# Seven block products instead of eight in both products of an MLP, with partial sums read out of PSUM between them

## The chip, the cores and the metric

One NeuronCore of a Trainium2 chip. The metric is the device time of one execution in microseconds. The kernel before takes 619.16 us (median of three runs, 618.53 to 621.18). Engines are called as the profile calls them: PE (TensorE), PEld (its weight loads), DVE (VectorE), ACT (ScalarE), POOL (GpSimd), SP (the queue that issues most transfers).

## The reference

An attention-like recurrence with a state of 48 x 48 for each head, followed by an MLP with a hardswish gate:

```python
# r, k, v, w: (4, 8, 768, 48) float32;  u: (8, 48)
for t in range(S):
    cur = einsum('bhd,bhe->bhde', u[None] * kt, vt)
    y[:, :, t] = einsum('bhd,bhde->bhe', rt, state + cur)
    state = wt[:, :, :, None] * state + einsum('bhd,bhe->bhde', kt, vt)

x = y.transpose(0, 2, 1, 3).reshape(3072, 384)
h = x @ w_in                                # (384, 2048)
g = h * clip(h + 3.0, 0.0, 6.0) / 6.0
out = g @ w_out                             # (2048, 384)
```

The MLP weights arrive as 64-bit floats and are converted to 32-bit floats on the chip. All products run in fp32.

## The kernel before

**Attention.** The 3072 tokens are 24 chunks of L = 128. For each chunk DVE runs two scans over the decays (`back_scan` L329, `fore_scan` L338); K and R are multiplied in by DVE for the first three chunks and by POOL afterwards (L349, L353). PE forms the scores (`score`, L384) into a PSUM tile of two banks, DVE copies the part above the diagonal into A (`above`, L390), PE reads state and values into another tile of the same kind (`read`, L435 and L452) and forms the state's update (L445). ACT takes the result out of PSUM (`leave`, L505 and L506) into xT, the transposed input of the MLP: three slices of 128 rows by the block's tokens. The fourth pair of heads goes through x3 and six small transfers (`last_pair`); in block 0 it goes through a product with a selection matrix instead (`read_last`, `read_rest`, L482).

**MLP.** BC = 3 chunks make a block (384 tokens, 8 blocks). `up` (L520) multiplies one of 16 slices of w_in (128 of the 2048 columns, three slices of depth) with the block's tokens: three products of 384 columns into one of three "mm" banks. ACT forms relu(h/6 + 1/2) from PSUM (`ramp`, L527), DVE takes min(r, 1) * h (`gate`, L534) into g. `down` (L542) multiplies, for each chunk, 16 slices of g with w_out: 16 products of 384 columns into an mm bank. ACT copies it out (`drain`, L548), SP stores it. Block 0 runs its up products in two parts, first for two chunks (256 columns) and then for one (128). Every fp32 product is two PE instructions in the profile, each with its own weight load.

**Start.** Weights come in 16 fetches of 768 KB (8 pairs of slices of w_in, then 8 of w_out). ACT does two and DVE three conversion steps for each (L298, L302, L307, L312, L317). Until the first up product PE is fed with products of the identity that nobody reads (`spin`, L743).

**Order.** The schedule is written by the program itself. `Plan.add` takes a step's name, engine, assumed duration, the steps that it comes after, a due time (key) and the ring buffers that it holds with the steps that free them. `Plan.order` walks through time: at each turn the engine that can start earliest takes, of its steps that are ready then, the one with the smallest key. The instructions are emitted in that order, and on the chip each engine works through its own list in it; waits follow from the data. A flag marks steps that use the SBUF port shared by DVE and POOL; the plan puts these one after the other. `START`, `CONV`, `UP`, `LAG` and `BEHIND` are the due times of the first chunks, of the conversion, of block 0's up products, the lead of a chunk before its block, and the fetches that the first chunks' loads stand behind. Later steps re-read inputs and check their ranges on DVE (`vet`); a second, general path runs only if such a check fails.

Of the kernel before, what the change touches and what calls it, by code (L numbers as in the profile page):

```python
# [30 lines left out]
UP = (-38.7, 1.8, -33.2, 2.0)  # L31
# [148 lines left out]
def fast_path(tc, feat, tok, wflat, ub, moe_w_in, moe_w_out, out, flag, n_chunks):  # L180
# [13 lines left out]
    MB = BC * L  # L194
    NB = NT // BC
# [3 lines left out]
    with ExitStack() as ctx:  # L199
# [12 lines left out]
        half = const.tile([128, 1], F32, name="half")  # L212
        ones = const.tile([128, 1], F32, name="ones")
        mask_f = const.tile([128, L], F32, name="mask_f")
# [5 lines left out]
        sel = const.tile([PR, NCC, 128], F32, name="sel")  # L220
        x3_0 = const.tile([PR, MB], F32, name="x3_0")
# [3 lines left out]
        def constants():  # L225
# [5 lines left out]
            nc.vector.memset(half, 0.5)  # L231
            nc.vector.memset(ones, 1.0)
            make_identity(nc, ident)

            nc.gpsimd.memset(mask_f, 1.0)
# [3 lines left out]

            nc.gpsimd.memset(x3_0, 0.0)  # L240
# [8 lines left out]
        plan.ring("tok", 4)  # L249
# [12 lines left out]
        def load_tok(i):  # L262
            b = io.tile([L, 3, HD], F32, name="tok_in", bufs=4)
            nc.sync.dma_start(out=b.rearrange("s c e -> s (c e)"), in_=tok[i].rearrange("s c e -> s (c e)"))
            st[i].update(rt=b[:, 0], kt=b[:, 1], v=b[:, 2].rearrange("s (h d) -> s h d", d=D))
# [55 lines left out]
        for r, k in (("E", 3), ("W", 3), ("rk", 2), ("dg", 2), ("A", 2), ("kn", 2), ("S", 2), ("x", 2), ("two", 2),  # L321
                     ("ps", 1), ("mm", 3), ("r6", 3), ("g", NFC + 3), ("o", 2)):
            plan.ring(r, k)
        w_min = const.tile([PR, NT, P], F32, name="w_min")

        def back_scan(i):
            d = st[i]
            E_ = wk.tile([PR, P * (L + 1)], F32, name="E", bufs=3)
# [6 lines left out]
        def fore_scan(i):  # L335
            d = st[i]
            W_ = wk.tile([PR, P * (L + 1)], F32, name="W", bufs=3)
# [20 lines left out]
        def own(i):  # L358
            d = st[i]
            d["rk"] = wk.tile([L, HD], F32, name="rk")  # L360
# [17 lines left out]
        def score(i):  # L378
            d = st[i]
            d["a_ps"] = pp.tile([128, 2, P, L], F32, name="two", bufs=2)  # L380
            for p in range(P):
                for g in range(2):
                    rows = slice(g * GP, g * GP + D)
                    nc.tensor.matmul(d["a_ps"][:, g, p, :], lhsT=d["K"][rows, p, :], rhs=d["R"][rows, p, :],  # L384
                                     start=True, stop=True)

        def above(i):

            d = st[i]
            nc.vector.copy_predicated(  # L390
                out=d["A"].rearrange("s (p g) t -> s g p t", g=2),
                mask=mask.rearrange("s (o x t) -> s o x t", o=1, x=1).to_broadcast([L, 2, P, L]),
                data=d["a_ps"])
# [61 lines left out]
        def new_y(i):  # L455
            st[i].update(started=set(), y_ps=pp.tile([128, 2, P, L], F32, name="two", bufs=2))
# [13 lines left out]
        def leave_last(i):  # L470
            if i == 0:
                blocks[0]["xT"] = wk.tile([128, NCC, MB], F32, name="xT")
            for g in range(2):
                rows = slice(g * GP, g * GP + D)
                nc.scalar.copy(out=x3_0[rows, i * L:(i + 1) * L], in_=st[i]["y_ps"][rows, 1, 0, :])

        def read_rest(i):
            d = st[i]
            begun = set()
            for j in range(NCC):  # L480
                bank, at = PLACES[j]
                nc.tensor.matmul(d["y_ps"][:, bank, at, :], lhsT=sel[:, j, :], rhs=x3_0[:, i * L:(i + 1) * L],  # L482
# [11 lines left out]
        def leave(i):  # L494
            bk, c = divmod(i, BC)
            b = blocks[bk]
            if c == 0:
                b["xT"] = wk.tile([128, NCC, MB], F32, name="xT")
                b["x3"] = wk.tile([PR, MB], F32, name="x3")
# [15 lines left out]
        def up(bk, f, c0, c1):  # L515
            b = blocks[bk]
            cols, m = slice(c0 * L, c1 * L), (c1 - c0) * L
            h_ps = b["h", f, c0] = pp.tile([128, MB], F32, name="mm", bufs=3)
            for j in range(NCC):
                nc.tensor.matmul(h_ps[:, :m], lhsT=w_in[:, f // 2, j, f % 2, :], rhs=b["xT"][:, j, cols],  # L520
                                 start=(j == 0), stop=(j == NCC - 1))

        def ramp(bk, f, c0, c1):
            b = blocks[bk]
            m = (c1 - c0) * L
            r6 = b["r", f, c0] = wk.tile([128, MB], F32, name="r6", bufs=3)
            nc.scalar.activation(out=r6[:, :m], in_=b["h", f, c0][:, :m], func=ACT.Relu, bias=half, scale=1.0 / 6.0)  # L527

        def gate(bk, f, c0, c1):
            b = blocks[bk]  # L530
            cols, m = slice(c0 * L, c1 * L), (c1 - c0) * L
            if c0 == 0:
                b["g", f] = wk.tile([128, MB], F32, name="g", bufs=NFC + 3)
            nc.vector.scalar_tensor_tensor(out=b["g", f][:, cols], in0=b["r", f, c0][:, :m], scalar=1.0,  # L534
                                           in1=b["h", f, c0][:, :m], op0=ALU.min, op1=ALU.mult)

        def down(bk, c, f0, f1):
            b = blocks[bk]
            if f0 == 0:
                b["o", c] = pp.tile([L, DM], F32, name="mm", bufs=3)  # L540
            for f in range(f0, f1):
                nc.tensor.matmul(b["o", c], lhsT=b["g", f][:, c * L:(c + 1) * L], rhs=w_out[:, f, :],  # L542
                                 start=(f == 0), stop=(f == NFC - 1))

        def drain(bk, c):
            b = blocks[bk]
            b["y", c] = wk.tile([L, DM], F32, name="o", bufs=2)
            nc.scalar.copy(out=b["y", c], in_=b["o", c])  # L548

        def store(bk, c):  # L550
            t0 = bk * MB + c * L
            nc.sync.dma_start(out=out[t0:t0 + L, :], in_=blocks[bk]["y", c])
# [13 lines left out]
        def refetch(which, j):  # L566
            if which == "w":
                t = io.tile([128, VN], F32, name="bits", bufs=3)
                nc.sync.dma_start(out=t, in_=wflat[:, j * VN:(j + 1) * VN])
            else:  # L570
                m = VN // 2
                t = io.tile([128, m], I64, name="bits", bufs=3)
# [42 lines left out]

        PB = NFC + BC * 4
        SUBS = ("", ".", "..")[:len(SPLIT) + 1], ("",)

        def when(i):

            bk, c = divmod(i, BC)
            return PB * bk - LAG - PB / BC * (BC - 1 - c)

        for i in range(NT):
            t = when(i)
            k = START[i] if i < len(START) else t - 14
# [8 lines left out]
            plan.add(f"back{i}", "DVE", 1.4, do(back_scan, i), [f"feat{i}"] + [f"fore{i - 2}"] * (i > 1), k,  # L635
# [12 lines left out]
            plan.add(f"diag0{i}", "ACT", 1.22, do(diagonal, i, 0), [f"sum{i}"], k + 0.6, [("A", [f"read{i}"])])  # L648
            plan.add(f"diag1{i}", "ACT", 1.22, do(diagonal, i, 1), [f"sum{i}", f"diag0{i}"], k + 0.6)

            due = k + 0.7 if i <= len(START) else when(i - 1) + 0.02
            t = k + 1 if i < len(START) else t
            plan.add(f"score{i}", "PE", 1.05, do(score, i), [f"K{i}", f"R{i}"], due, [("two", [f"above{i}"])])
            plan.add(f"above{i}", "DVE", 1.3, do(above, i), [f"score{i}", f"diag1{i}"], due + 0.5)
# [12 lines left out]
            space = [("x", [f"up{bk}.{f}{x}" for f in range(NFC) for x in SUBS[bk > 0]])] if c == 0 else []  # L667
            if bk == 0:
                plan.add(f"first{i}", "PE", 0.35 + 0.3 * (not first), do(read_last, i), [f"above{i}"] + reads[2:], t + 0.01,
                         [("two", [f"leave{i}"])])  # L670
                plan.add(f"third{i}", "ACT", 0.55, do(leave_last, i), [f"first{i}"], t + 0.01, space)
# [3 lines left out]
            else:  # L675
                plan.add(f"read{i}", "PE", 1.0 + 0.45 * turn + 0.5 * (not first), do(read, i), reads
                         + [f"up{j}.{NFC - 1}{SUBS[j > 0][-1]}" for j in (bk - 2,) if j >= 0],
                         t + 0.01, [("two", [f"leave{i}"])] + [("ps", [f"state{i}"])] * turn)
                plan.add(f"leave{i}", "ACT", 1.46, do(leave, i), [f"read{i}"], t + 0.5, space)
                if c == BC - 1:  # L680
                    for g in range(2):
                        plan.add(f"move{bk}.{g}", "SP", 1.8, do(last_pair, bk, 0, BC, g, nc.sync),
# [399 lines left out]
```

## Time and profile before

| | |
|---|---|
| median of three runs | 619.16 us |
| the profiled execution | 618.55 us, its span 616.7 us |
| PE busy | 602.4 us, 98% of the span |
| PE busy in L520 and L542 (up, down) | 254.7 and 251.6 us |
| DVE, ACT, POOL busy | 270.7, 215.6, 126.5 us |
| mean granted clock of PE | 0.997 |

How to read it: the page gives busy time by engine, forty slices of the span with the busy share in tenths, and the chain of work that ended last. A row of a group has the line, the engine, the operation, the tiles, the shape, the count, then the busy time and the mean of one instruction, then the idle time of the engine just before it and what ended that. PE's records overlap, since a product's record is longer than the distance to the next one: a price for PE is read from a run of products without a gap, not from the mean of a record.

### The profile page before, as it was taken

The numbers are of one execution on the slowest core, as the hardware profiler recorded it, in microseconds if no ns is written. First come the engines' busy times: TensorE is split into PE (matmuls) and PEld (weight loads), VectorE is DVE, ScalarE is ACT, GpSimd is POOL, SyncE is SP. The second block draws the span as 40 slices with busy tenths as digits, with TensorE's granted clock in tenths as the row PEclk, the third lists the DMA queues.
The fourth block names the chain that finished last, engine by engine and source line by source line (L and its number), as shares of the span: only waits on it lengthen the run. The fifth ranks groups of instructions, "written<-read, shape, count | busy, mean of one in ns | idle before, by whom it ended". The sixth has DMA issues, their size and how long they took to land.

```text
span 616.7 us, 8184 instructions
## 1 busy us (share of the span) xinstructions
PE 602.4 (98%) x3262; PEld 386.4 (63%) x3262; DVE 270.7 (44%) x395; ACT 215.6 (35%) x530; POOL 126.5 (21%) x119
## 2 busy tenths in 40 slices
PE   7899999999999999999999999999999999999996
PEld 7778756666566566566565665665666666555553
DVE  6999995665152661455541652224601231002200
ACT  3778915534032441243231440324402431112200
POOL 3114057723031230231230320202301000000000
PEclk9999999999999999999999999999999999999998
DMA  8969646762243523362263620300100000000000
GB/s 296 304 200 325 208 124 189 231 219 84 80 142 128 174 83 121 100 219 90 76 203 108 210 80 19 106 18 34 40 14 22 14 1 0 23 26 2 1 13 30
DMA packets 20190, 67.16 MB, mean 109 GB/s; under 512 B 2464, under 2 KB 6336, under 8 KB 20144
## 3 DMA queue, kind: packets, MB, share of 16 engines
q1 hardware_dynamic: 19872, 65.91, 32.8%
q10 hardware_dynamic: 272, 0.66, 0.4%
q8 instruction: 27, 0.44, 0.3%
q14 instruction: 19, 0.16, 0.1%
HBM read 60.81 MB, written 4.72 MB: 106 GB/s over the span
## 4 chain that ended last, share of the span: by engine, by line
PE 89%; DVE 7%; DMA 1%; ACT 1%; issue 1%; SPq 0%; DVEq 0%; ACTq 0%
PE mm L542 39%; PE mm L520 38%; PE two L384 4%; PE two L452 3%; PE two L435 2%; PE ps L445 2%; PE ps L399 2%; DVE top L312 1%; DMA tok_in<-in_tok_dram 1%; DVE top L307 1%; DVE w_in L317 1%; DVE w_out L317 1%; DVE E L349 1%; DVE g L534 1%; DVE E L329 0%
## 5 line engine op out<-in xcount | busy, mean ns | idle before, releaser
L520 PE MATMUL mm<-xT,w_in 128*128 128x384 f32 (+2 forms) x864 | 254.7, 453 | 1.7 <-DVE g L534 1.5
L542 PE MATMUL mm<-w_out,g 128*128 128x384 f32 x768 | 251.6, 487 | 0.5 <-DVE w_out L317 0.5
L520 PEld LDWEIGHTS mm<-xT,w_in 128*128 128x128 f32 x864 | 155.6, 190 | 91.8 <-DVE g L534 3.3
L542 PEld LDWEIGHTS mm<-w_out,g 128*128 128x128 f32 x768 | 144.9, 190 | 100.0 <-DVE w_out L317 1.1
L534 DVE SCALAR_TENSOR_TENSOR g<-r,mm 128x384 f32<-128x384 f32 (+2 forms) x144 | 72.5, 508 | 207.9 <-ACT r L527 207.8
L527 ACT ACTIVATE r<-mm,half 128x384 f32<-128x384 f32 (+2 forms) x144 | 77.8, 543 | 134.5 <-PE mm L520 133.0
L416 POOL TENSOR_TENSOR S<-state,E 112x192 f32<-112x192 f32 x18 | 21.2, 1179 | 247.9 <-DVE state L411 209.9
L548 ACT COPY o<-mm 128x384 f32<-128x384 f32 x24 | 11.5, 478 | 162.9 <-PE mm L542 160.5
L376 ACT ACTIVATE A<-ident,dg 128x128 f32<-128x128 f32 x192 | 60.4, 390 | 3.7 <-DVE dg L368 3.4
L505 ACT COPY xT<-two 48x384 f32<-48x384 f32 x42 | 19.8, 472 | 72.9 <-PE two L452 72.5
L338 DVE TENSOR_TENSOR_SCAN W<-feat_in,start 112x516 f32<-112x516 f32 x24 | 31.5, 1314 | 28.1 <-PE two L435 28.0
L353 POOL TENSOR_TENSOR W<-feat_in,W 112x512 f32<-112x512 f32 x21 | 27.4, 1303 | 61.8 <-DVE W L338 61.8
L390 DVE COPY_PREDICATED A<-mask,two 128x1024 f32<-128x1024 uint8 x24 | 31.3, 1307 | 15.8 <-PE two L384 15.8
L362 POOL TENSOR_TENSOR rk<-tok_in 128x384 f32<-128x384 f32 x23 | 24.5, 1066 | 49.4 <-DMA tok_in<-in_tok_dram 41.2
L329 DVE TENSOR_TENSOR_SCAN E<-feat_in,back 112x516 f32<-112x516 f32 x24 | 31.3, 1306 | 3.4 <-DMA feat_in<-in_feat_dram 3.4
L349 POOL TENSOR_TENSOR E<-feat_in,E 112x512 f32<-112x512 f32 x21 | 27.6, 1313 | 21.1 <-issue 8.6
L384 PE MATMUL two<-W,E 48*128 48x128 f32 x384 | 27.6, 284 | 0.8 <-DVE W L353 0.8
L452 PE MATMUL two<-A,tok_in 128*48 128x128 f32 x384 | 27.7, 275 | 0.3 <-DVE A L390 0.3
L384 PEld LDWEIGHTS two<-W,E 48*128 48x128 f32 x384 | 23.2, 187 | 6.5 <-issue 4.2
L411 DVE TENSOR_TENSOR state<-S,ps 112x192 f32<-112x192 f32 x16 | 5.6, 351 | 46.0 <-PE ps L445 45.5
L363 POOL TENSOR_TENSOR rk<-rk,u_bc 128x384 f32<-128x384 f32 x23 | 24.8, 1080 | 1.8
L452 PEld LDWEIGHTS two<-A,tok_in 128*48 128x48 f32 x384 | 21.1, 123 | 1.7 <-issue 0.9
(61 smaller groups left out, 280.0 us busy)
## 6 DMA issues: line engine op xcount, KB each, us to landing
feat_in<-in_feat_dram SPq DMA_DIRECT2D x23, 674.2 KB, 5.7
tok_in<-in_tok_dram SPq DMA_DIRECT2D x24, 576.0 KB, 3.8
bits<-in_moe_w_in_dram SPq DMA_DIRECT2D x16, 768.0 KB, 6.5
bits<-in_moe_w_out_dram SPq DMA_DIRECT2D x16, 768.0 KB, 5.7
out_dram<-o SPq DMA_DIRECT2D x24, 192.0 KB, 1.9
bits<-in_wflat_dram SPq DMA_DIRECT2D x6, 768.0 KB, 6.1
xT<-x SPq DMA_DIRECT2D x42, 24.0 KB, 1.9
feat_in<-in_feat_dram ACTq DMA_DIRECT2D x1, 448.0 KB, 5.2
```

The source lines that it names most:

```text
L329: nc.vector.tensor_tensor_scan(out=E_[:, ::-1], data0=d["w"][:, :0:-1], data1=back.rearrange("q p t -> q (p t)")[:, ::-1], initial=0.0, op ...
L338: nc.vector.tensor_tensor_scan(out=W_, data0=d["w"][:, :-1], data1=starts[i % 2].rearrange("q p t -> q (p t)"), initial=0.0, op0=ALU.mult, ...
L349: early(i).tensor_mul(d["K"], d["k"], d["K"])
L353: early(i).tensor_mul(d["R"], d["r"], d["R"])
L376: nc.scalar.activation(out=d["A"][:, h, :], in_=ident, func=ACT.Copy, scale=d["dg"][:, h])
L384: nc.tensor.matmul(d["a_ps"][:, g, p, :], lhsT=d["K"][rows, p, :], rhs=d["R"][rows, p, :], start=True, stop=True)
L390: nc.vector.copy_predicated(out=d["A"].rearrange("s (p g) t -> s g p t", g=2), mask=mask.rearrange("s (o x t) -> s o x t", o=1, x=1).to_br ...
L452: nc.tensor.matmul(lhsT=d["v"][:, 2 * p + g, :], rhs=d["A"][:, 2 * p + g, :], stop=True, **into(i, p, g))
L520: nc.tensor.matmul(h_ps[:, :m], lhsT=w_in[:, f // 2, j, f % 2, :], rhs=b["xT"][:, j, cols], start=(j == 0), stop=(j == NCC - 1))
L527: nc.scalar.activation(out=r6[:, :m], in_=b["h", f, c0][:, :m], func=ACT.Relu, bias=half, scale=1.0 / 6.0)
L534: nc.vector.scalar_tensor_tensor(out=b["g", f][:, cols], in0=b["r", f, c0][:, :m], scalar=1.0, in1=b["h", f, c0][:, :m], op0=ALU.min, op1= ...
L542: nc.tensor.matmul(b["o", c], lhsT=b["g", f][:, c * L:(c + 1) * L], rhs=w_out[:, f, :], start=(f == 0), stop=(f == NFC - 1))
```

## The change

Blocks become four chunks (BC = 4, 512 tokens, 6 blocks). Block 0 keeps the ordinary products, its up products in two halves of two chunks (256 columns each). From block 1 on, both MLP products are formed as 2 x 2 blocks by seven block products instead of eight (Winograd's form).

*Up*: the 2 x 2 blocks are two neighbouring slices of w_in's columns (a row pair q, eight of them) by the first two slices of depth, and by the two halves of the block's tokens. The third slice of depth is added to the products in the ordinary way. A row pair has eleven products of 256 columns. *Down*: for each half p of the block (two chunks), the blocks are the two chunks by the two halves of the 2048 depth, and by the two halves of the 384 output columns: seven products, each over eight slices, of 192 columns.

The sums of weight blocks are formed once, on DVE (`sum_in`, `sum_out`), under block 0, partly in place of the weights; the sums of xT (`sum_x`) and of g (`sum_g`) on DVE in each block. Several products are accumulated in the same PSUM bank, and partial sums are read out in between: `s1` after product 1, `u` after 6, `v` after 5 (ACT copies), `c11`, `c12`, `c22` (DVE, bank plus what was copied before), `c21` at the end (ACT). Clip and gate then work on 512 columns in SBUF; the factor 1/6 moves to the reads of the down product.

PSUM is divided anew: bankA (2), bankB (1), bankC (2) of one bank each, y (two banks), ps (one). A chunk's score uses bankB and a bankC, and `above` becomes two instructions. Rings get smaller (E, W, tok, rk), the re-reads use the buffers of `feat`, and the order is planned with new durations and due times.

```diff
-BC = 3
+BC = 4
...
-LAG = 6
-BEHIND = (-1, -1, 0, 3, 6, 8)
+LAG = 19.1
+BEHIND = (-1, -1, 0, 3, 5, 8)
-SPLIT = (2,)
-START = (-52.0, -52.0, -39.0, 6.5, 11.0, 7.6)
-CONV = (-45.0, 3.3)
-UP = (-38.7, 1.8, -33.2, 2.0)
+START = (-104.5, -104.0, -78.0, -38.2, 22.0, 30.0)
+CONV = (-90.0, 6.6)
+UP = (-83.9, 3.6, -69.0, 4.3)
+SUMS = (36.2, 2.0)
...
+        def sum_x(bk, part):
...
+            for o, x, y in (((T[:, 0], b12, b11), (T[:, 1], b22, T[:, 0])),
+                            ((b12, b22, b12), (T[:, 2], b21, T[:, 1]), (T[:, 3], c1, c2)))[part]:
+                nc.vector.tensor_tensor(out=o, in0=x, in1=y, op=ALU.subtract)
+
+        def up_product(bk, q, k):
...
+            to, terms = {
+                1: ("A", [(w_in[:, q, 0, 0, :], x[:, 0, one])]),
+                5: ("C", [(a_slot(0, q), T[:, 0])]),
+                2: ("B", [(w_in[:, q, 1, 0, :], x[:, 1, one]), (w_in[:, q, 2, 0, :], x[:, 2, one])]),
+                6: ("A", [(a_slot(1, q), T[:, 1])]),
+                3: ("C", [(a_slot(2, q), x[:, 1, two]), (w_in[:, q, 2, 0, :], x[:, 2, two])]),
+                7: ("A", [(w_in[:, q, 0, 1, :], x[:, 0, two]), (w_in[:, q, 2, 1, :], x[:, 2, two])]),
+                4: ("A", [(w_in[:, q, 1, 1, :], T[:, 2]), (w_in[:, q, 2, 1, :], T[:, 3])]),
+            }[k]
+            for n, (w, rhs) in enumerate(terms):
+                nc.tensor.matmul(b["p", q, to][:, :HB], lhsT=w, rhs=rhs, start=(n == 0 and k in (1, 2, 5)),
+                                 stop=(n == len(terms) - 1 and k in (2, 3, 4)), skip_group_check=True)
+
+        def up_read(bk, q, what):
...
+            if what in ("s1", "u", "v", "c21"):
+                nc.scalar.copy(out=to, in_=src)
+            else:
+                nc.vector.tensor_add(to, src, to)
+
+        def up_ramp(bk, q, p):
+            clip(bk, p, blocks[bk]["g", p][:, 2 * q:2 * q + 2, :].rearrange("p f t -> p (f t)"), ("r", q, p))
+
+        def up_gate(bk, q, p):
...
+            nc.vector.scalar_tensor_tensor(out=g, in0=b["r", q, p], scalar=6.0, in1=g, op0=ALU.min, op1=ALU.mult)
+
+        def sum_g(bk, p, k, x):
...
+            o, x0, x1, op = {1: (S, a21, a22, ALU.add), 2: (S, S, a11, ALU.subtract), 3: (a21, a11, a21, ALU.subtract),
+                             4: (S, a12, S, ALU.subtract)}[k]
+            nc.vector.tensor_tensor(out=o, in0=x0, in1=x1, op=op)
...
+                for k_, us, key, after, hold in (
+                        (1, 1, 0, [], [("bankA", [r + "c21"])]), (5, 1, 1, [], [("bankC", [r + "c12"])]),
+                        (2, 2, 2.1, [], [("bankB", [r + "c11"])]), (6, 1, 4, [r + "s1"], []), (3, 2, 5, [r + "v"], []),
+                        (7, 2, 7, [r + "u"], []), (4, 2, 13.05, [r + "c22"], [])):
...
+                for what, eng, after, key in (("s1", "ACT", [u + "1"], 1), ("v", "ACT", [u + "5"], 2), ("u", "ACT", [u + "6"], 5),
+                                              ("c11", "DVE", [u + "2", r + "s1"], 4), ("c12", "DVE", [u + "3", r + "u"], 7),
+                                              ("c22", "DVE", [u + "7", r + "v"], 9), ("c21", "ACT", [u + "4"], 15)):
...
+                for n_, (k_, after, hold) in enumerate((
+                        (1, [], [("bankA", [r + "c21"])]), (2, [], [("bankB", [r + "c11"])]), (5, [], [("bankC", [r + "c12"])]),
+                        (6, [r + "s1"], []), (3, [r + "v"], []), (7, [r + "u"], []), (4, [r + "c22"], []))):
```

In the table of `(k_, us, key, after, hold)` the second and third entries are a product's length and due time in units of one product of 256 columns; product 4 is due at 13.05, that is after products 1 and 5 of the next row pair.

More of the change, by code (lines that the diff above doesn't have):

```diff
@@ L389, in above @@
             d = st[i]
[L390 to L393, printed above, removed]
+            for g in range(2):
+                nc.vector.copy_predicated(
+                    out=d["A"].rearrange("s (p g) t -> s g p t", g=2)[:, g],
+                    mask=mask.rearrange("s (x t) -> s x t", x=1).to_broadcast([L, P, L]),
+                    data=d["a_ps"][g])
         def turn_k(i):
@@ new lines, in fast_path @@
+        all_down = [x for d_ in downs for x in d_]
+        for n_, (t_, x) in enumerate((t_, x) for t_ in (1, 2, 4, 3) for x in range(2)):
+            before = [f"sout{y}.{x}" for y in ({2: (1,), 4: (2,)}.get(t_, ()))] + [f"sout{t_}.0"] * x
+            if t_ == 3:
+                before += all_down + [f"sout1.{x}"]
+            if t_ == 1 and x == 0:
+                before += [f"{ready}{len(pairs) - 1}"]
+            plan.add(f"sout{t_}.{x}", "DVE", 0.95, do(sum_out, t_, x), before, SUMS[0] + 4 * SUMS[1] + n_ * SUMS[1] / 2,
+                     [("bits", ["end"])] * (t_ != 3 and x == 0), port=True)
```

371 lines of the change are left out of this document (263 added, 108 removed).

## The prediction

> **What bounds the kernel now.** I read the page first (busy shares, slices, chain), then the busy time by stretch, then the chain in order of time and the groups by shape. The page:
>
> ```profile
> span 616.7 us, 8184 instructions
> PE 602.4 (98%) x3262; PEld 386.4 (63%) x3262; DVE 270.7 (44%) x395; ACT 215.6 (35%) x530; POOL 126.5 (21%) x119
> PE   7899999999999999999999999999999999999996
> DVE  6999995665152661455541652224601231002200
> PEclk9999999999999999999999999999999999999998
> PE 89%; DVE 7%; DMA 1%; ACT 1%; issue 1%; SPq 0%; DVEq 0%; ACTq 0%
> ```
>
> TensorE (PE) is busy in 98% of the span at the full granted clock, and the chain lies on it for 89%. Busy time alone could be idle pipeline, so the stretches of the first 100 us and of one later block (three chunks) come next (columns: stretch, length, then PE, PEld, DVE, ACT, POOL, clock, DMA share, GB/s):
>
> ```profile
> 0.00:50.00 50.00, 43.28 (x395) 37.98 (x396) 44.12 (x67) 29.70 (x65) 12.23 (x21) 1.00 0.83 277
> 50.00:100.00 50.00, 48.00 (x294) 35.27 (x293) 44.44 (x67) 32.17 (x75) 19.75 (x15) 1.00 0.66 203
> 261.07:333.50 72.43, 72.43 (x382) 44.86 (x381) 32.72 (x46) 23.51 (x61) 17.02 (x15) 1.00 0.40 129
> ```
>
> From the second block on PE never idles, while DVE works 32.72 of 72.43 us and ACT 23.51. Only PE work counts there. At the start PE and DVE are both nearly full: DVE converts weights. The prices of PE's passes (each fp32 product appears as two instructions, "passes") come from the chain in order of time (start, length) and the timeline:
>
> ```profile
> 33.92 3.90 PE mm L520 x18
> 580.17 30.97 PE mm L542 x96
> 23.21 2.50 PE L743 MATMUL mm<-ident 128*128 128x128 f32 x20
> L743 PE MATMUL mm<-ident 128*128 128x128 f32 x122 | 17.5, 305 | 1.4 <-POOL ident masks.py:199 1.4
> L520 PE MATMUL mm<-xT,w_in 128*128 128x384 f32 x672 | 220.7, 487 | 0.0
> L520 PE MATMUL mm<-xT,w_in 128*128 128x256 f32 x96 | 23.4, 385 | 0.3 <-DVE g L534 0.2
> L542 PE MATMUL mm<-w_out,g 128*128 128x384 f32 x768 | 251.6, 487 | 0.5 <-DVE w_out L317 0.5
> L520 PEld LDWEIGHTS mm<-xT,w_in 128*128 128x128 f32 x864 | 155.6, 190 | 91.8 <-DVE g L534 3.3 <-issue 0.4 <-DVE state L411 0.2
> ```
>
> A 384-column pass takes 30.97 / 96 = 0.3226 us, a 256-column pass (the L520 passes at 33.92 are of that form) 3.90 / 18 = 0.2167, a 128-column pass (2.50 − 0.305) / 19 = 0.116, the last record taken off. The mean of a record (487 ns) is longer than its pitch, because passes overlap. So a block of three chunks spends 2 × 30.97 = 61.9 us on the MLP and the rest of 72.43, 10.5 us or 3.5 us a chunk, on attention.
>
> **The change, part by part.**
>
> *Products.* The down products use 192 columns, a width that the trace doesn't have. The line through 256 and 384 gives 0.2167 − 64 × (0.3226 − 0.2167)/128 = 0.164; half-way between 128 and 256 lies 0.166. I take 0.164. The MLP of four chunks cost 4/3 × 61.9 = 82.6 us. After: up 8 row pairs × 11 products × 2 passes = 176 × 0.2167 = 38.1; down 2 halves × 7 × 8 × 2 = 224 × 0.164 = 36.7; together 74.8. Gain 7.8 a block, 39 us over blocks 1 to 5. The up product can gain only a twelfth (11 products instead of 12), because a third of its depth stays ordinary; the down product gains nearly its eighth, less 0.6 us for narrower passes (36.7 against 7/8 × 41.3 = 36.1).
>
> *Block 0* stays ordinary, with 192 passes of 256 (41.6) and 128 of 384 (41.3): 82.9 us for four chunks. Before, three chunks took 96 × 0.2167 + 96 × 0.116 + 30.97 = 62.9. Against 4/3 of 61.9 this is +0.3, and the old surplus of 1.0 goes: net −0.7. A fourth chunk takes block 0's attention route with the selection product, six more passes of 0.116: +0.7. These two cancel.
>
> *Attention* on PE is unchanged, 24 × 3.5 us. PSUM is split anew, and a chunk's score holds the single bankB and one of two bankC until the masked copy has read them. The rows of the copy, and of one read and the score after it:
>
> ```profile
> L390 DVE COPY_PREDICATED A<-mask,two 128x1024 f32<-128x1024 uint8 x24 | 31.3, 1307 | 15.8 <-PE two L384 15.8
> 92.79 0.66 PE L435 MATMUL two<-W,S 48*48 48x128 f32 x16
> 94.85 1.16 PE L384 MATMUL two<-W,E 48*128 48x128 f32 x16
> ```
>
> The copy (1.31 us) runs beside the read of the chunk ahead, 94.85 − 92.79 = 2.06 us on PE, so I cost it at nothing; without that cover 20 scores would lose up to 1.3 us each, 26 us.
>
> *Reads out of PSUM between products.* This is the new wait. In each row pair product 7 needs ACT's copy `u` after product 6, with product 3 (four passes, 0.867 us) between; product 4 needs DVE's sum `c22` after 7, with the next pair's products 1 and 5 (0.867 us) between. The round trip from rows:
>
> ```profile
> L475 ACT COPY x<-two 48x128 f32<-48x128 f32 x6 | 1.6, 259 | 3.5 <-PE two L452 3.4
> L548 ACT COPY o<-mm 128x384 f32<-128x384 f32 x24 | 11.5, 478 | 162.9 <-PE mm L542 160.5 <-DMA xT<-x 2.4
> L534 DVE SCALAR_TENSOR_TENSOR g<-r,mm 128x256 f32<-128x256 f32 x16 | 6.6, 414 | 1.3 <-ACT r L527 1.2
> 38.10 0.43 PE L452 MATMUL two<-A,tok_in 128*48 128x128 f32 x4
> 38.60 0.53 ACT L475 COPY x<-two 48x128 f32<-48x128 f32 x2 [0.27 <-PE two L452]
> 26.07 0.34 DVE L416 TENSOR_TENSOR S<-state,E 112x192 f32<-112x192 f32 x1
> 26.56 0.42 PE L435 MATMUL two<-W,S 48*48 48x128 f32 x4 [0.85 <-DVE S L416]
> ```
>
> A record outlives its slot by 0.385 − 0.217 = 0.17 us; PE's end to ACT's start is 38.60 − 38.53 = 0.07; a 256-column copy lies half-way between 0.259 and 0.478, 0.37; DVE's end to PE's start is 26.56 − 26.41 = 0.15. That makes 0.76 through ACT and 0.80 through DVE (0.414 for the sum): hidden with 0.07 to 0.1 us to spare if the engine is free at that moment. If it isn't, the longest ordinary instruction ahead counts:
>
> ```profile
> L527 ACT ACTIVATE r<-mm,half 128x384 f32<-128x384 f32 x112 | 64.8, 579 | 128.9 <-PE mm L520 128.8
> L534 DVE SCALAR_TENSOR_TENSOR g<-r,mm 128x384 f32<-128x384 f32 x112 | 62.0, 554 | 206.0 <-ACT r L527 206.0
> L338 DVE TENSOR_TENSOR_SCAN W<-feat_in,start 112x516 f32<-112x516 f32 x24 | 31.5, 1314 | 28.1 <-PE two L435 28.0
> L353 DVE TENSOR_TENSOR W<-feat_in,W 112x512 f32<-112x512 f32 x3 | 2.0, 676 | 0.0
> ```
>
> The clip and gate on 512 columns extend these by one step of 128 (0.109 and 0.14 us from the rows of 256 and 384): about 0.69 each. A clip ahead of `u` costs 0.69 − 0.1 = 0.6 us, a gate ahead of `c22` 0.6, a scan 1.2. Queued behind a late ACT copy are the other copies and clips, behind a late DVE sum the gates and scans. So a row pair loses between 0 and 1.2 us. Against the upper end speak two things: PE's order is written from a plan that moves the next pair's 1, 5 and 2 (1.7 us, with a second bankA and bankC) ahead of a product that isn't ready; and the loads are moderate. DVE per block of four: 24 sums × 0.414 = 9.9, 16 gates × 0.69 = 11.0, 16 sums of g × 0.676 = 10.8, 11 sums of x and of the outputs of at most 0.414, about 4, attention 4/3 × (32.72 − 16 × 0.554) = 31.8; 67.5 us of 88.8. ACT: 32 copies × 0.37, 16 clips × 0.69, 8 output reads of 0.3, and 4/3 × (23.51 − 16 × 0.579 − 3 × 0.478) = 17.1 for attention; 42 of 88.8. I take 0.1 us a pair, near the bare round trip: 40 pairs, 4 us. In a down half a sum of g (0.676 us, with the hops 0.17 + 0.07 + 0.15 about 1.07) stands between two half products of 8 × 0.164 = 1.3 us: hidden again, unless a scan is ahead (then 1.1 us). I take 0.3 us for each of ten halves, 3 us.
>
> *Weight sums* for block 1 on are 16 of 256 columns and 8 of 768 on DVE; at 0.676 us for 512 columns that is at most 16 × 0.4 + 8 × 1.0 = 14 us. They run under block 0's down products (41.3 us on PE, with four chunks' attention beside).
>
> *Start.* The rows of the conversion:
>
> ```profile
> 55.06 0.96 DVE L317 CUSTOM_DVE_ANT_0 w_in<-top,more 128x1536 uint16<-128x1536 uint16 x1
> 81.26 0.96 DVE L317 CUSTOM_DVE_ANT_0 w_out<-top,more 128x1536 uint16<-128x1536 uint16 x1
> 82.14 1.23 DVE L338 TENSOR_TENSOR_SCAN W<-feat_in,start 112x516 f32<-112x516 f32 x1
> L353 POOL TENSOR_TENSOR W<-feat_in,W 112x512 f32<-112x512 f32 x21 | 27.4, 1303 | 61.8 <-DVE W L338 61.8
> ```
>
> PE starts the first up product at 33.9 in either case. Half 0 of block 0 is then 20.8 us, with chunks 2 and 3 about 7: to 62. w_in is ready at 56.0, but half 1 now needs chunk 3's attention, whose forward scan came at 82.14 in the old order and must now come before w_out's conversion. Wholly behind w_in, chunk 3's chain (scan 1.3, product on POOL 1.3, score 1.1, copy 1.3, read 2.1, leaving about 1: 8 us) ends at 64, so PE idles 2 us, and up to 8 where other DVE work goes first; well placed, nothing. Half 1 (20.8 us) then lies beside w_out's conversion (56.0 to 82.2 in the old rows), of which the first down products need only the first pairs. I take 2 us.
>
> *Tail.* In the last half, product 4 waits for `c22` with nothing left to fill it: 0.76 us. What follows the last product (copy, store) stays.
>
> *Sum* against the profiled execution's own 618.55 us (0.6 below the median): −39 + 0 + 4 + 3 + 2 + 0.8 = −29.2, so 589.
>
> A rule speaks against the change. The Trainium skill, "TensorE: Matmul & The Clock Gate", under "What overlaps and what doesn't" in Part 3, says that a weight load overlaps with running products only when it goes to another row group. Here all loads fill all rows, so by that rule every pass would pay for its load, and by it the sum would be that of the rival on loads below, 673. This case's trace disagrees: 384 columns pass every 0.3226 us, and 128 columns with a load each every 0.116 us, although a load's record lasts 0.190.
>
> **Rivals.**
>
> - *Reads late now and then* (half the cover lost): 0.4 to 0.5 us a pair, 16 to 20 us instead of 4: 601 to 605. For it: ACT and DVE are queues with 0.7 to 1.3 us instructions in them. Against it: the filling above.
> - *Start starved*: chunk 3 behind the conversions, 8 us or more instead of 2, and block 0 ends late as DVE has 44.44 of 50 us taken: 597 to 605.
> - *Reads late at every pair* (slower): both waits find the long instruction ahead, 1.16 us × 40 = 46, and each down half 1.1: 618.55 − 39 + 46 + 11 + 3 = 640. It decides from 0.6 us a pair on (24 us, beside 14 of the other losses). For it: one wrong place in a fixed order repeats in all 40 pairs. Against it: at most 76% load on DVE and 47% on ACT.
> - *The load shows* (slower): were the loads not hidden, 5 × (400 − 4/3 × 192) = 720 more of them at up to 0.116 us (a 128-column pass with its load) would cost 84 us: 673. The 128-column row speaks against it.
> - *Better*: no losses at all, 618.55 − 39 = 579.5.
>
> **How the numbers follow.** Forecast (580 to 598) 0.65, better than 580 0.03, late now and then 0.13, start starved 0.07, late at every pair 0.07, the load 0.02, and 0.03 for a mixture that ends at no change. A measurement of this kernel tells about 0.5% (3 us) from no change. Faster: 0.65 + 0.03 + 0.13 + 0.07 = 0.88; same 0.03; slower 0.09. The range runs from no losses (580) to the upper end of "now and then" (608).
>
> **What would show it.** Right: PE busy about 40 us shorter, up passes of 256 at 0.217 and down passes of 192 near 0.164 in back-to-back runs, a block of four in 88 to 91 us instead of 96.6, idle time before products 7 and 4 of some 0.1 us a pair. Wrong: idle of PE released by ACT's copies or DVE's sums of over 0.5 us a pair; a gap of PE between 56 and 70 us that ends with chunk 3; a 192-column pitch above 0.2 us.

## The result and the profile after

The changed kernel takes 584.94 us (median of four runs, 583.17 to 585.48) beside 618.85 us for the kernel before on the same chip (618.47 to 621.18): a ratio of 0.944, interval 0.941 to 0.947. That is 34 us faster, 4 us below the forecast and inside its range. The profiled execution took 583.17 us, its span 581.5.

The page of the changed kernel, beside that of before:

```profile
PE 566.4 (97%) x3940; PEld 495.5 (85%) x3940; DVE 402.6 (69%) x666; ACT 265.5 (46%) x677; POOL 128.1 (22%) x119
PE 92%; DVE 4%; ACT 1%; DMA 1%; issue 1%; DVEq 0%
```

PE is 36 us less busy (602.4 to 566.4) though it has 678 more instructions, and it still carries the chain. DVE rises from 270.7 to 402.6 us, and after block 0 PE waits for it only once, for 0.3 us. The stretches at the start, and one later block, now of four chunks (the columns are those of the prediction's stretches):

```profile
0.00:50.00 50.00, 46.50 (x383) 40.00 (x384) 43.07 (x69) 29.91 (x66) 11.72 (x22) 1.00 0.86 282
50.00:100.00 50.00, 44.10 (x244) 34.07 (x243) 44.55 (x69) 32.88 (x69) 15.16 (x12) 0.97 0.51 169
243.30:330.60 87.30, 87.30 (x659) 79.36 (x659) 67.01 (x110) 39.90 (x107) 24.33 (x21) 1.00 0.46 146
```

A block of four takes 87.3 us, where four chunks took 96.6 before, with PE full. DVE works 67.0 us of it and ACT 39.9. The start is different: between 50 and 100 us PE was busy for 48.00 us before and is for 44.10 now. The passes, from the chain in order of time (start, length):

```profile
250.63 2.16 PE bankA L634 x10
302.83 6.50 PE bankA L681 x40
567.05 9.11 PE bankA L681 x56
```

An up pass of 256 columns takes 2.16/10 = 0.216 us and a down pass of 192 columns 6.50/40 = 0.1625. The last row is the end of the kernel: 56 passes at 9.11/56 = 0.1627, so the last product 4 does not wait either. All waits of PE that the view of waits lists (who waits, for whom, us in all, times, longest):

```profile
PE bankC L536 <- DVE w_in L320: 3.7, 1, 3.7
PE bankA L552 <- DVE w_out L320: 1.6, 1, 1.6
PE bankA L980 <- POOL ident masks.py:199: 1.4, 1, 1.4
PE ps L404 <- DVE E L353: 1.4, 1, 1.4
PE y_ps L487 <- ACT x L480: 1.3, 2, 0.7
PE bankA L634 <- DVE g L645: 0.3, 1, 0.3
```

Only the last line belongs to the reads between products: one wait of 0.3 us in forty row pairs and ten down halves. The rest lies in the start and block 0.

**Where the time went.** I added up PE's passes from start to start in both traces and compared each MLP pass with its pitch (0.3226, 0.216, 0.1625 us, and for the 128-column up passes of before 0.109, the shortest distance between two of them). The MLP at pitch falls from 495.7 to 454.8 us, by 40.9. What MLP passes took above the pitch rises from 7.9 to 13.0 us, by 5.1, which is the wait of 3.7 us and the slow passes behind it. Attention and selection products behind the first up product rise from 73.4 to 79.5, by 6.1; the wait of 1.6 us is in here, since a score stands ahead of it, and so are the two waits for ACT's x. The first up product starts 5.1 us earlier. Together −40.9 + 5.1 + 6.1 − 5.1 = −34.8; PE's last pass ends at 576.15 instead of 611.13, 35.0 earlier. The last two terms belong together in part. Before, chunk 0's score was late and chunk 2's score still came ahead of the first up product; after, it comes behind, with 1.5 us for it and the four products after it. PE's rows of the kernel before:

```profile
16.57 2.06 PE L384 MATMUL two<-W,E 48*128 48x128 f32 x32 [0.79 <-DVE W L353]
31.07 1.16 PE L384 MATMUL two<-W,E 48*128 48x128 f32 x16
33.75 2.55 PE L520 MATMUL mm<-xT,w_in 128*128 128x256 f32 x11
```

and of the changed kernel (the first rows of the scores of chunk 0 and chunk 2, each with 15 more like it behind):

```profile
11.17 0.37 PE L388 MATMUL bankB<-W,E 48*128 48x128 f32 x1
28.62 1.56 PE L536 MATMUL bankC<-xT,w_in 128*128 128x256 f32 x6
31.41 0.37 PE L388 MATMUL bankB<-W,E 48*128 48x128 f32 x1
```

### The profile page after: what moved, and what is told of

Read it like the earlier page. It is cut to its first block, busy times and chain, and to the rows that moved or that the text cites. A ratio compares the mean times of both kernels' runs of the same rounds, so it can differ in the third digit from the quotient of the medians.

```text
span 581.5 us, 10098 instructions
## 1 busy us (share of the span) xinstructions
PE 566.4 (97%) x3940; PEld 495.5 (85%) x3940; DVE 402.6 (69%) x666; ACT 265.5 (46%) x677; POOL 128.1 (22%) x119
## 4 chain that ended last, share of the span: by engine, by line
PE 92%; DVE 4%; ACT 1%; DMA 1%; issue 1%; DVEq 0%
PE bankA L634 18%; PE bankA L681 17%; PE bankC L634 9%; PE bankC L681 9%; PE bankA L552 7%; PE bankB L634 6%; PE bankB L681 4%; PE y_ps L457 4%; PE bankB L388 4%; PE bankC L536 4%; PE bankA L536 3%; PE y_ps L440 2%; PE ps L450 2%; PE ps L404 1%; PE bankA L980 1%; DMA feat_in<-in_feat_dram 1%
## 5 line engine op out<-in xcount | busy, mean ns | idle before, releaser
L643 ACT COPY g<-bankA 128x256 f32<-128x256 f32 x120 | 44.5, 371 | 51.7 <-PE bankA L634 49.3
L653 DVE SCALAR_TENSOR_TENSOR g<-clip,g 128x512 f32<-128x512 f32 x80 | 56.7, 712 | 9.8 <-ACT clip L526 9.8
L526 ACT ACTIVATE clip<-g,three 128x512 f32<-128x512 f32 x80 | 57.9, 723 | 11.4 <-DVE g L645 10.7
L634 PE MATMUL bankA<-xT,w_in 128*128 128x256 f32 x240 | 60.9, 380 | 0.0
L681 PE MATMUL bankA<-w_out,g 128*128 128x192 f32 x320 | 56.8, 328 | 0.0
L681 PEld LDWEIGHTS bankA<-w_out,g 128*128 128x128 f32 x320 | 52.5, 190 | 1.0 <-issue 0.4
L634 PEld LDWEIGHTS bankA<-xT,w_in 128*128 128x128 f32 x240 | 44.9, 190 | 6.1 <-issue 0.4
L552 PE MATMUL bankA<-w_out,g 128*128 128x384 f32 x128 | 44.4, 494 | 1.6 <-DVE w_out L320 1.6
L634 PE MATMUL bankB<-xT,w_in 128*128 128x256 f32 x160 | 41.3, 380 | 0.0
L357 POOL TENSOR_TENSOR W<-feat_in,W 112x512 f32<-112x512 f32 x21 | 27.3, 1302 | 57.1 <-DVE W L342 24.7
L552 PEld LDWEIGHTS bankA<-w_out,g 128*128 128x128 f32 x128 | 23.4, 190 | 16.6 <-DVE w_out L320 1.8
L634 PEld LDWEIGHTS bankB<-xT,w_in 128*128 128x128 f32 x160 | 30.2, 190 | 4.3 <-DVE g L653 0.2
```

The source lines that it names most:

```text
L526: nc.scalar.activation(out=c[:, :m], in_=src, func=ACT.Relu, bias=three, scale=1.0)
L552: nc.tensor.matmul(b["o", c][:, :DM], lhsT=b["g", c // 2][:, f, c % 2 * L:(c % 2 + 1) * L], rhs=w_out[:, f, :], start=(f == 0), stop=(f == ...
L634: nc.tensor.matmul(b["p", q, to][:, :HB], lhsT=w, rhs=rhs, start=(n == 0 and k in (1, 2, 5)), stop=(n == len(terms) - 1 and k in (2, 3, 4) ...
L643: nc.scalar.copy(out=to, in_=src)
L653: nc.vector.scalar_tensor_tensor(out=g, in0=b["r", q, p], scalar=6.0, in1=g, op0=ALU.min, op1=ALU.mult)
L681: nc.tensor.matmul(b["d", p, to][:, :h], lhsT=a, rhs=w(), start=(f == 0 and k in (1, 2, 5)), stop=(f == HF - 1 and k in (2, 3, 4)), skip_g ...
```

## The experiments

My theory after the result: the gain is the number of passes times their pitch, nothing else; the reads cost nothing because the written order puts more between a read and its user than the prediction assumed; what is lost lies at the start. Rivals: part of the gain comes from the new blocks and PSUM tiles themselves; the reads are covered by speed, not by order; the start's waits could be moved away.

| kernel | median, us | range | ratio to before (interval) |
|---|---|---|---|
| the changed kernel | 584.94 | 583.17–585.48 | 0.944 (0.941–0.947) |
| ordinary products, all else as changed | 625.89 | 624.95–628.64 | 1.010 (1.008–1.012) |
| only the up products by seven | 608.80 | 607.89–608.97 | 0.983 (0.980–0.985) |
| only the down products by seven | 602.29 | 599.90–602.83 | 0.971 (0.969–0.974) |
| next pair's products not ahead | 617.58 | 616.19–620.80 | 0.996 (0.995–0.998) |
| later reads, the plan knows | 586.11 | 585.75–586.55 | 0.947 (0.945–0.949) |
| later reads, the plan doesn't know | 593.52 | 591.99–593.90 | 0.958 (0.956–0.960) |
| identity products in the first gap | 584.38 | 582.75–588.21 | 0.944 (0.942–0.946) |
| identity products in both gaps | 583.87 | 583.45–584.85 | 0.943 (0.942–0.945) |
| chunk 3 loaded later | 594.07 | 592.93–598.60 | 0.962 (0.959–0.965) |
| chunk 3 loaded earlier | 589.19 | 588.18–589.83 | 0.951 (0.948–0.953) |
| chunks 4 and 5 loaded later | 588.83 | 587.42–590.61 | 0.951 (0.948–0.954) |

### The products apart from the rest

The first kernel keeps blocks of four, the new PSUM tiles, rings, due times and block 0, but forms all products in the ordinary way, without sums and reads. The next two put back one of the two products.

```diff
-                    plan.add(u + str(k_), "PE", 0.43 * us, do(up_product, bk, q, k_),
...
+            for p in range(2):
+                for f in range(NFC):
+                    n_, at = f"{bk}.{f}.{p}", K + (NFC * p + f) * 1.29
+                    plan.add(f"up{n_}", "PE", 1.29, do(up, f, p, bk),
...
-                        plan.add(d_ + f"{k_}.{x}", "PE", 1.3, do(down_product, bk, p, k_, x),
...
+            for c in range(BC):
+                for q in range(HF):
+                    plan.add(f"down{bk}.{c}.{q}", "PE", 1.29, do(down, c, 2 * q, 2 * q + 2, bk),
```

> All blocks use the ordinary eight products in the new layout (blocks of four, the new PSUM banks, start and due times; no sums of weights, x or g, no reads between products). Theory: the whole gain is PE's pass time, 5 x (41.3 - 38.0) for up and 5 x (41.3 - 36.4) for down = 41 us by the pitches of the profile after, and the rest of the change costs some 5 us (the start). So 622 to 628. Rival: the new blocks, banks and start bring part of the 34 us themselves; then below 615.

> Only the up product by seven, down ordinary. Theory: 5 x 3.3 = 16.5 us below the kernel with all products ordinary, so 606 to 611. Rival (the reads between the up products cost several us that the down product's gain hides): less than 10 us below it.

> Only the down product by seven, up ordinary. Theory: 5 x 4.9 = 24.5 us below the kernel with all products ordinary, so 598 to 603, and the two parts add up to the whole change. Rival (sums of g stand between half products and cost): less than 20 us below it, and the parts do not add up.

Measured on one chip, with 620.71 us for the kernel before: 625.89, 608.80 and 602.29 us. The up products by seven bring 625.89 − 608.80 = 17.1 us, the down products 23.6; together 40.7, and the whole change brings 41.0 against the first kernel (584.94 us, measured beside a kernel before that took 1.9 us less). So the parts add to within that difference, and the gain is the products'. All else costs 625.89 − 620.71 = 5.2 us, and its trace has the same two waits as the changed kernel:

```profile
PE bankC L536 <- DVE w_in L320: 3.7, 1, 3.7
PE bankA L552 <- DVE w_out L320: 1.6, 1, 1.6
```

They belong to the new start, not to the reads or the sums. Part of the 5.2 us may be a slow clock: in this trace the granted clock was 0.50 for 3.4 us behind the first of these gaps and for 10 us behind the second, and the kernel's runs go from 624.95 us at a mean clock of 0.995 to 628.64 at 0.988.

### What covers the reads

Here products 1, 5 and 2 of a row pair may no longer go ahead of product 4 of the pair before; the instructions are the same. The plan then also draws product 3 ahead of 6 in 24 of the 40 pairs (in 4 of the changed kernel's), so that in 23 no up product stands between 6 and 7 either.

```diff
-                        (7, 2, 7, [r + "u"], []), (4, 2, 13.05, [r + "c22"], [])):
+                        (7, 2, 7, [r + "u"], []), (4, 2, 9, [r + "c22"], [])):
...
-                        order_ = order_ + [f"up{bk}.{q - 1}.{k_}"]
+                        order_ = order_ + [f"up{bk}.{q - 1}.{k_}"] + [f"up{bk}.{q - 1}.4"] * (k_ in (1, 5, 2))
```

> Products 1, 5 and 2 of a row pair are ordered behind product 4 of the pair before, nothing else changed. Theory (the next pair's products cover the read of c22, a round trip of 0.80 us by the rows of the first profile): up to 0.8 us a pair shows, 32 us less what attention fills, so 597 to 617, with PE's idle time in front of product 4. Rival (the reads are short enough or PE's queue hides them without that order): within 4 us of the changed kernel, 583 to 589.

Measured 617.58 us, 32.6 more than the changed kernel: nearly the whole gain is gone. PE's waits:

```profile
PE bankA L634 <- DVE g L645: 10.4, 19, 1.1
PE bankA L634 <- ACT g L643: 5.0, 11, 0.5
PE bankA L681 <- ACT g L643: 2.3, 5, 0.5
```

One exposed read, in the timeline (product 7, the sum `c22`, product 4):

```profile
278.58 1.13 PE L634 MATMUL bankA<-xT,w_in 128*128 128x256 f32 x4
279.77 0.41 DVE L645 TENSOR_TENSOR g<-bankA,g 128x256 f32<-128x256 f32 x1
280.23 1.13 PE L634 MATMUL bankA<-T__2052,w_in 128*128 128x256 f32 x4 [0.53 <-DVE g L645]
```

The idle time in brackets is counted from the end of the last record, which outlives its slot by 0.17 us; so the bare trip costs 0.53 + 0.17 = 0.70 us of PE here. Over all waits it is 10.4/19 + 0.17 = 0.72 through DVE and 5.0/11 + 0.17 = 0.62 through ACT, where the prediction had worked out 0.80 and 0.76. Added up from start to start, the up passes of blocks 1 to 5 lie 33.9 us above their pitch instead of 2.5: 31.4 us, 0.78 a row pair. The trip is nearly as long as thought, then, and it is the order that hides it. How, a row pair of the changed kernel shows (timeline; attention and weight loads left out):

```profile
268.03 0.59 PE L634 MATMUL bankA<-T__2061,top 128*128 128x256 f32 x2
268.23 0.80 ACT L643 COPY g<-bankA 128x256 f32<-128x256 f32 x2 [0.43 <-PE bankA L634]
...
268.46 0.59 PE L634 MATMUL bankC<-xT,more 128*128 128x256 f32 x2
...
268.89 0.59 PE L634 MATMUL bankC<-xT,w_in 128*128 128x256 f32 x2
...
269.32 0.59 PE L634 MATMUL bankC<-T__2061,more 128*128 128x256 f32 x2
...
269.75 1.46 PE L634 MATMUL bankA<-xT,w_in 128*128 128x256 f32 x6
...
271.05 1.03 PE L634 MATMUL bankB<-xT,w_in 128*128 128x256 f32 x4
271.25 0.42 DVE L645 TENSOR_TENSOR g<-bankA,g 128x256 f32<-128x256 f32 x1 [0.59 <-PE bankA L634]
...
271.91 0.59 PE L634 MATMUL bankA<-T__2061,top 128*128 128x256 f32 x2
...
272.34 0.38 PE L634 MATMUL bankA<-T__2061,w_in 128*128 128x256 f32 x1
```

Product 6 is the row at 268.03. Behind it come 3 (268.46 and 268.89), the next pair's 5 (269.32) and, as the first two of the six passes at 269.75, its 1; product 7 starts at about 270.18. That is 1.72 us behind the end of 6; the second copy of the ACT row, `u`, ends at 269.03, 1.15 us early. Behind 7 come the next pair's 2 (271.05) and 6 (271.91), 1.29 us, before product 4 at 272.34; `c22` ends at 271.67, 0.67 us early. The prediction had 0.867 us at both places.

This pair is not one of the tight ones. Counted over the 40 pairs of the trace, 17 have 0.863 us between 6 and 7, product 3 alone, just as predicted; one of them:

```profile
161.24 0.59 PE L634 MATMUL bankA<-T__1385,more 128*128 128x256 f32 x2
161.44 0.80 ACT L643 COPY g<-bankA 128x256 f32<-128x256 f32 x2 [0.55 <-PE bankA L634]
161.68 0.59 PE L634 MATMUL bankC<-xT,more 128*128 128x256 f32 x2
162.11 0.59 PE L634 MATMUL bankC<-xT,w_in 128*128 128x256 f32 x2
162.54 1.46 PE L634 MATMUL bankA<-xT,w_in 128*128 128x256 f32 x6
```

Here product 7 starts at 162.54, 0.86 us behind the end of 6, and `u` still ends at 162.24, 0.3 us early. Between 7 and 4 six pairs have no more than 0.863 us, and `c22` ends 0.24 us early there. So a longer cover is not what hides all the reads. In the tight pairs the bare cover is enough because the engine is free when the product ends: in the trace ACT starts `u` 0.03 us behind the end of product 6 in 37 of the 40 pairs, and DVE `c22` on average 0.24 us behind the end of 7.

### How much delay the order takes

Two extra copies on ACT ahead of each `u` and a reduction on DVE ahead of each `c22`, of data that nobody needs; in the first kernel the plan knows of them, in the second the order is that of the changed kernel.

```diff
+        def pad(what):
+            if what == "u":
+                for _ in range(2):
+                    nc.scalar.copy(out=pad_a[:, 0, :], in_=w_in[:, 0, 2, :, :].rearrange("p a b -> p (a b)"))
+            else:
+                nc.vector.tensor_reduce(out=pad_d, in_=w_in[:, 0:2, 2, :, :], axis=AX.XYZ, op=ALU.max)
...
+                    if what in ("u", "c22"):
+                        plan.add(r + "pad" + what, eng, 0.7, do(pad, what), after, at + 0.43 * key - 4.01, [])
+                        after = after + [r + "pad" + what]
```

In the second kernel the last three lines are `fn = (lambda w=what, f=fn: (pad(w), f()))` instead.

> In each row pair ACT does two copies of 256 columns that nobody reads ahead of u, and DVE a reduction of 512 elements ahead of c22 (about 0.7 and 0.6 us), and the plan that writes PE's order knows of them; DVE and ACT have 24 to 28 us more work each in all. Theory (the order, with the next pair's products pulled ahead, is what covers the reads): within 6 us of the changed kernel, 583 to 591. Rival (the cover is a fixed 0.87 us, as the prediction priced it): 0.6 us for each late read, 40 x 1.2 = 48 us, so about 630.

> The same extra instructions, but the plan doesn't know of them, so PE's order is that of the changed kernel. Theory (the order is laid out to the real durations, with little slack besides): 0.4 to 0.6 us for each late read, 30 to 48 us, so 615 to 633. Rival (the order has slack of its own, so that late reads cost nothing either way): within 6 us of the changed kernel.

Measured 586.11 us with the plan, 1.2 more and not to be told from the changed kernel, as expected; and 593.52 without it, 8.6 more. The second number falls between what theory and rival expected, so both had a size wrong. In the second kernel's trace the additions take this (groups by shape), and PE waits so:

```profile
L335 ACT COPY pad_a<-w_in 128x256 f32<-128x256 f32 x80 | 32.4, 405 | 1.3
L337 DVE TENSOR_REDUCE pad_d<-w_in 128x1 f32<-128x512 f32 x40 | 27.0, 676 | 0.0
```

```profile
PE bankA L643 <- ACT g L652: 3.3, 18, 0.2
PE bankA L643 <- DVE g L654: 0.9, 1, 0.9
```

The additions take 0.81 us on ACT and 0.68 on DVE in each pair, but the reads are not that much later: the additions don't read the products, so an engine that would sit idle does them beforehand. In this trace `u` starts 0.62 us behind the end of product 6 in most pairs instead of 0.03, and `c22` on average 0.56 us behind the end of 7 instead of 0.24. So the test delays them by some 0.59 and 0.32 us. Who pays is plain from the pairs: the 17 with product 3 alone between 6 and 7 grow from 0.863 to 1.206 us there, 17 × 0.343 = 5.8 us of the 8.6; of the stretches between 7 and 4 only one grows. With 0.07 to 0.1 us to spare everywhere, as the prediction had it, these delays would have cost an estimated 40 × (0.59 − 0.1 + 0.32 − 0.07), some 30 us.

### The start

Six passes behind the 3.7 us gap ran at half speed (the granted clock is 0.50 from 53.7 to 57.1 us; timeline of the changed kernel; first the up passes, then the first down passes):

```profile
54.16 2.93 PE L536 MATMUL bankC<-xT,w_in 128*128 128x256 f32 x6 [3.66 <-DVE w_in L320]
56.88 1.58 PE L536 MATMUL bankA<-xT,w_in 128*128 128x256 f32 x6
64.10 1.56 PE L552 MATMUL bankA<-w_out,g 128*128 128x384 f32 x4 [1.58 <-DVE w_out L320]
```

The same six passes take 2.93 us, then 1.58. I filled the gap with 15 products of the identity that nobody reads, and in another kernel also the second gap with nine.

```diff
+                if (f, p) == (12, 0):
+                    plan.add("fill", "PE", 0.0, fill, [f"up0.{f - 1}.0"], k, [("bankA", ["fill"])])
+                    wait = ["fill"]
...
+                if c == q == 0:
+                    plan.add("fill2", "PE", 0.0, lambda: fill(9), [f"up0.{NFC - 1}.0", "score3"], k, [("bankA", ["fill2"])])
+                    wait = ["fill2"]
```

> 15 products of the identity that nobody reads are put in front of block 0's up product 12 of the first half, where PE idled 3.66 us and the six passes after it took 0.21 us longer each at a halved granted clock. Theory (the idle time lowers the clock, and passes at the lower clock cost 6 x 0.21 = 1.3 us): 1.0 to 1.6 us faster, 583.3 to 584. Rival (the slow passes have to do with the late weights, not with idle time): no change, 584.5 to 585.5.

> As with the spins in the gap at 50 us, and 9 more of these products in front of block 0's first down product, where PE idles about 2 us for w_out's first pair; in the run with the first gap filled the granted clock was halved after this second one. Theory (idle time of some 2 us or more halves the clock for a while, in some executions after the first gap and in some after the second): with both filled no pass is slow, 581.5 to 583.8, and the runs lie closer together. Rival (the clock isn't moved by these gaps, or the spins cost as much as they save): 584.3 to 585.5 as before.

Measured 584.38 us (five runs, 582.75 to 588.21) with the first gap filled, no change; its profiled execution was its slowest run, and its timeline says why:

```profile
54.51 1.56 PE L536 MATMUL bankC<-xT,w_in 128*128 128x256 f32 x6 [0.33 <-DVE w_in L320]
63.51 2.42 PE L552 MATMUL bankA<-w_out,g 128*128 128x384 f32 x4 [2.08 <-DVE w_out L320]
72.69 2.34 PE L552 MATMUL bankA<-w_out,g 128*128 128x384 f32 x4
```

The up passes now run at full speed; but this time the second gap, 2.08 us, left the down passes slow (2.42 us for four instead of 1.56), and still 9 us later. With both gaps filled no slow pass is in the trace, the mean clock is 0.999, and the runs lie closer together (583.45 to 584.85); the median is 583.87, 1.1 us below the changed kernel's and not clear of its noise. By these medians the slow clock would cost about 1 us on the whole; PE's wait for the data stays.

Three kernels moved the loads of the chunks among the weight fetches (`BEHIND` is the list of fetches that the chunks' loads stand behind):

```diff
-BEHIND = (-1, -1, 0, 3, 5, 8)
+BEHIND = (-1, -1, 0, 6, 7, 8)
...
+BEHIND = (-1, -1, 0, 2, 5, 8)
...
+BEHIND = (-1, -1, 0, 3, 8, 10)
```

The third also orders `u` of each block's first row pair behind its `v`, so its number is not that of the loads alone.

> The loads of chunks 3, 4 and 5 stand behind fetches 6, 7 and 8 instead of 3, 5 and 8. Theory (the wait of 3.66 us at 50 us is for the landing of w_in's pair 6, queued behind chunk 3's 1.25 MB): the wait goes, with the slow passes after it, 3 to 5 us, and chunk 3 comes late enough to give part back: 580 to 584. Rival (PE is short of work there whichever comes first): 585 to 590.

> Chunk 3's loads stand behind fetch 2 instead of 3; chunks 4 and 5 as in the changed kernel. Theory (PE waits at 50 us for the landing of the late pairs of w_in, which share the transfers with chunk 3): chunk 3 lands before the late pairs are asked for, so the wait shrinks, 580 to 584. Rival (the buffers of the weight fetches come free by DVE's pace, whatever is loaded between): no change, 584 to 586.

> Chunks 4 and 5 are loaded behind fetches 8 and 10 instead of 5 and 8; chunk 3 as in the changed kernel. Theory (late pairs of weights share the transfers with the chunk loads asked for at 45 us): the waits for w_in and w_out, 3.7 and 1.6 us, shrink: 581 to 584. Rival (chunks 4 and 5 come late for block 1 and PE waits for them instead): 587 or more.

All three theories missed: 594.07, 589.19 and 588.83 us, 4 to 9 us slower than the changed kernel. Only the third one's rival (587 or more) has the time right. With chunk 3 later, PE's waits are

```profile
PE bankA L552 <- DVE w_out L320: 5.5, 1, 5.5
PE bankA L536 <- DVE g L544: 3.4, 1, 3.4
PE bankC L536 <- DVE w_in L320: 3.3, 1, 3.3
```

and with chunks 4 and 5 later

```profile
PE bankA L552 <- DVE w_out L320: 3.1, 1, 3.1
PE bankB L388 <- POOL W L357: 1.8, 1, 1.8
PE ps L450 <- ACT kn L409: 1.3, 1, 1.3
PE bankC L536 <- DVE w_in L320: 0.3, 1, 0.3
```

The wait for w_in does go in the last one, from 3.7 to 0.3 us, but others take its place. DVE works 43.07 and 44.55 of the first two 50 us, and the transfers are busy for 0.86 of the first: a step moved there pushes another. Which of them sets the start stays open: a kernel that was to give chunk 2's two products to POOL, to relieve DVE, gave no result. No kernel here beats the changed one clearly.

## Why the prediction was right

- *Products*: −39 predicted, −40.9 at pitch in the trace, −40.7 from the two parts alone. The width that no row showed, 192 columns, was put at 0.164 us and is 0.1625. The narrower passes make up most of the difference: 5 × 224 × (0.164 − 0.1625) = 1.7 us.
- *Weight loads*: hidden, as the 128-column row had said. A load's record lasts 0.190 us, a 192-column pass every 0.1625; the rule of the Trainium skill that the prediction weighed ("TensorE: Matmul & The Clock Gate", Part 3, "What overlaps and what doesn't"; 673 by it) does not hold in this kernel.
- *Reads between products*: +4, +3 and +0.8 predicted, 0.3 us of waits measured. This is the term that was mis-sized. Its trip was nearly right (0.80 and 0.76 worked out, about 0.7 and 0.62 measured), and its cover was right for 17 reads of `u` and six of `c22`; elsewhere the written order has more, 1.72 and 1.29 us in the pair first shown, as the prediction's own argument on the plan had it. The charges of 0.1 us a pair and 0.3 a down half were for an engine being late, and where the cover was short it was free. The 0.76 us at the tail were charged because nothing seemed left to fill with; but the plan held product 4 of the last block's first half back until behind the last product 7 (570.79 to 573.4 us), and it covers the last `c22` (570.99 to 571.35). The loads of DVE and ACT in a block were right: 67.5 and 42 predicted, 67.0 and 39.9 measured. "Late at every pair" was to decide from 0.6 us a pair on: the kernel without the cover loses 0.78 a pair and ends at 0.996 of before, about where that rival turns.
- *Start*: +2 predicted, and not where I put it. PE idles before the first up product of the thirteenth slice at 50.5 to 54.2 us, for w_in, and then at 62.5 to 64.1 us for w_out; no gap ends with chunk 3. A slow clock adds about 1 us, as far as the noise lets that be seen. I had taken the first up product as fixed at 33.9; it starts at 28.62, because chunk 0's score comes 5.4 us earlier (16.57 to 11.17). All that is not products costs 5.2 us by the kernel with ordinary products, the slow clock included.
- *Sum*: 9.8 us of losses predicted (4 + 3 + 2 + 0.8) against some 6 in the trace (−40.9 of products, −34.8 in all). With the products 2 us better, the time came out 4 us below the forecast: right in its mechanism, with a loss too high at the reads and too low at the start. The upper end of its range, 608, is not the end of the rival that it names for it (605).

## What to carry to other kernels

A scheme with fewer products is worth its pass count times the pitch of its shapes, to within 2 us here, if each partial sum is read while other products run. Count that cover in the order in which the instructions are written, and ask whether the reading engine is free at that moment: 0.62 us of trip was free behind 0.86 us of products with ACT idle, cost 0.34 us when ACT came 0.59 us late, and without products in between the reads cost nearly the whole gain. In three tries at this start, where PE, DVE and the transfers are all nearly full, moving loads moved the wait and did not remove it.

## What the hardware showed that I had not expected

After an idle stretch of 1.6 to 3.7 us PE's passes can take twice as long for about 3 to 10 us: six passes of 256 columns 2.93 us instead of 1.58 after a gap of 3.66 us, four of 384 columns 2.42 instead of 1.56 after one of 2.08. Which gap does it varies between executions: in the changed kernel's trace the second gap (1.58 us) left the clock alone, and in that of the kernel with ordinary products one of 1.57 us was followed by 10 us at a granted clock of 0.50 (four passes of 384 columns 2.25 us right behind it and 2.51 us 9 us later). By the Trainium skill, "TensorE: Matmul & The Clock Gate", Part 1, "What's actually happening", the clock drops to half after an idle window of about 3.4 us that runs freely, not started anew with a kernel. The halving, and that it follows the same gap in one execution and not in another, agree with these rows; but here 1.57 us of idle time was enough, less than half of that.
